# Attention with 16 queries a head: K of a block in one load of 64 KB rows, its last 28 tokens through a buffer of their own

## The chip, the core and the metric

The kernel runs on one core of a Trainium2 chip. The metric is device time in microseconds (us), the median of the runs; a profiled execution has a span, from its first to its last instruction. The engines are PE (TensorE, with PEld for its weight loads), DVE (VectorE), ACT (ScalarE), POOL (GpSimd) and SP (SyncE, which here only issues DMAs).

## The reference

For each of 8 x 16 = 128 heads there are 16 queries, 2048 keys and 2048 values of 256 numbers each, all in bf16.

```python
B, H, Sq, Skv, Dh = 8, 16, 16, 2048, 256
scores = jnp.einsum('bhqd,bhkd->bhqk', q, k) * q.shape[-1] ** -0.5
attn = softmax(scores, axis=-1)
out = jnp.einsum('bhqk,bhkd->bhqd', attn, v)
```

## The kernel before

**Blocks.** Eight heads make a block, so there are G = 16 blocks. K of a block is 8 MB, V as well. SBUF holds one block of K and one of V (the tile `SL`, four slots of 64 tokens a partition: `VA`, `VB` for V, `KA`, `KB` for K). V of a block comes as 128 tokens a partition, 16 partitions to a head, in rows of 64 KB. K comes in two halves of four heads, each 64 tokens a partition, 32 partitions to a head, in rows of 32 KB and loads of 4 MB. K of block 0 goes to V's slots, K of block 1 to K's.

**One block.** DVE transposes K in place, 32 tokens of all 256 numbers at a time (`kt`, line 200, 128x4096 words of 4 bytes). PE multiplies it with zero-padded query weights `QW` into `S_ps` (`qk`, lines 296 and 297: 296 with a weight load, 297 without). DVE takes the maximum (222), ACT the exponential (282), DVE transposes the result twice (226, 227), and DVE and ACT copy it into `PTz`, padded (207, 209 and 269). PE then multiplies it with V (`pv`, 317, "PV" below), and ACT writes the scaled result (262).

**Order.** Each engine has its own loop, written out by hand, over the blocks. PE's loop does QK of block r, 20 spare matmuls into `X_ps` that are used nowhere, and PV of block r-1. DVE's does the softmax of block g and the transposes of K of block g+1. Block 0 has its own QK loop ahead (328 to 337).

**Loads.** SP issues all DMAs on one queue, in program order, each behind a wait until its place is free: a half of K waits for the QK of that half of the block before it (`c_qk` grows by 4 a half, 8 a block), V for the end of the PV of the block before it (`c_pv`, 8 a block). The order is K halves of block j, then V of block j-1 (148 to 152); ahead of that loop, blocks 0 to 2 are written out (134 to 147), V of blocks 0 and 1 in halves. K and V of the last blocks come in smaller pieces (`PIECES`).

Of the kernel before, what the change touches and what calls it, by code (L numbers as in the profile page):

```python
# [5 lines left out]
ALU = mybir.AluOpType  # L6
# [4 lines left out]
SP = mybir.EngineType.SP  # L11
BF16 = mybir.dt.bfloat16
F32 = mybir.dt.float32

T = 64
SPARE = 5
# [4 lines left out]
def bass_standalone__softmax_full_bidir__sampling_kernel(  # L21
# [16 lines left out]
    ku = k.rearrange("b h s d -> (b h s) d").rearrange("(u p t) d -> u p t d", p=128, t=T)  # L38
# [4 lines left out]
    with ExitStack() as es:  # L43
        ec = es.enter_context
        SL = ec(nc.sbuf_tensor("SL", [128, 4, T, D], BF16))
        QT = ec(nc.sbuf_tensor("QT", [128, SQ * D], BF16))
# [19 lines left out]
        def sem(name):  # L66
            return ec(nc.semaphore(name))
# [3 lines left out]
        s_k = [sem("s_ka"), sem("s_kb")]  # L71
        s_kl = [sem("s_kla"), sem("s_klb")]
        s_v = sem("s_v")
        s_v0 = sem("s_v0")
# [6 lines left out]
        c_kt = [sem("c_kt0"), sem("c_kt1")]  # L81
# [10 lines left out]

        SLf = SL[:].bitcast(F32)

        QX = PTz[:, 1, 0:SQ * D // 128, :].rearrange("p t m -> p (t m)")

        QXu = QX.rearrange("p (c u a y) -> p a u c y", u=8, a=4, y=2)

        QTu = QT[:].rearrange("p (c u y) -> p u c y", u=32, y=2)

        SLk = SL[:].rearrange("p s (c t) (b i q) -> p s c b q t i", t=16, i=32, q=2)

# [5 lines left out]
        VW = SL[:, VA:VB + 1, :, :].rearrange("p a t d -> p (a t) d")  # L108


# [9 lines left out]
        def qx(Q, a):  # L120

            return (QTu[32 * a:32 * a + 32, 8 * Q:8 * Q + 8, :, :].rearrange("p u c y -> p c u y"),
                    QXu[32 * Q:32 * Q + 32, a, :, :, :].rearrange("p u c y -> p c u y"))

        def load_k(eng, g, e, slot, t0, n, s):
            eng.dma_start(SL[:, slot, t0:t0 + n, :], ku[2 * g + e, :, t0:t0 + n, :]).then_inc(s, 16)  # L126

        def on_sync(eng):
            def load_v(w, a, n):

                eng.wait_ge(c_pv, 8 * w + (a + n + C - 1) // C)
                eng.dma_start(VW[:, a:a + n, :], vb[w, :, a:a + n, :]).then_inc(s_p[a] if a else s_v, 16)  # L132

            eng.dma_start(QX, qh).then_inc(s_q, 16)
            for g, s0, s in ((0, VA, s_k0), (1, KA, s_k)):
                for e in range(2):
                    load_k(eng, g, e, s0 + e, 0, T, s[e])

            for e in range(2):
                eng.wait_ge(c_qk, 4 * e + 4)  # L140
                eng.dma_start(VW[:, T * e:T * e + T, :], vb[0, :, T * e:T * e + T, :]).then_inc(s_v0 if e else s_v, 16)
            for e in range(2):
                eng.wait_ge(c_qk, 4 * e + 12)
                load_k(eng, 2, e, KA + e, 0, T, s_k[e])
            for e in range(2):
                eng.wait_ge(c_pv, 4 * e + 12)
                eng.dma_start(VW[:, T * e:T * e + T, :], vb[1, :, T * e:T * e + T, :]).then_inc(s_v0 if e else s_v, 16)
            with nc.Fori(3, last, engines=[SP], hint_back_edge=True) as j:
                for e in range(2):
                    eng.wait_ge(c_qk, 8 * j + 4 * e - 4)  # L150
                    load_k(eng, j, e, KA + e, 0, T, s_k[e])
                load_v(j - 1, 0, 2 * T)
            for e in range(2):
                eng.wait_ge(c_qk, 8 * last + 4 * e - 4)
                load_k(eng, last, e, KA + e, 0, T // 2, s_k[e])
                load_k(eng, last, e, KA + e, T // 2, T // 2, s_kl[e])
            for w in PIECES:
                for a, n in PIECES[w]:
                    load_v(w, a, n)
            eng.wait_ge(c_ev, G)  # L160
            eng.dma_start(oh[:, 0:last, :], O_all[:, 2:G + 1, :]).then_inc(s_st, 16)
            eng.wait_ge(c_ev, G + 1)
            eng.dma_start(oh[:, last, :], O_all[:, G + 1, :]).then_inc(s_st, 16)
            eng.wait_ge(s_st, 32)

        def on_gpsimd(eng):

            for x, n in ([(c_pv, 8)] + [(x, 1) for x in s_kl] +
                         [(s_p[a], 16 * G - 16 * sum(a in dict(PIECES[w]) for w in PIECES)) for a in s_p]):
                eng.sem_inc(x, n)  # L170
# [18 lines left out]
            eng.memset(zero[1], 0.0).then_inc(c_pool, 1)  # L189

        def on_vector(eng):
# [6 lines left out]
            def kt(e, h, slot, n=1, first=False):  # L198
                x = SLf[:, slot, 32 * h:32 * h + 32 * n, :].rearrange("p t i -> p (t i)")
                eng.transpose(x, x).then_inc(c_k0 if first else c_kt[e], n)  # L200
# [11 lines left out]
            for e in range(2):  # L212
                eng.wait_ge(s_k0[e], 16)
                for h in range(2):
                    kt(e, h, VA + e, 1, True)

            eng.wait_ge(s_k[0], 16)
            kt(0, 0, KA, 2)
            eng.wait_ge(c_pool, 2)
            with nc.Fori(0, G, engines=[DVE]) as g:  # L220
# [8 lines left out]
                mid = eng.to_reg((g + 15) & 15)  # L229
                with eng.If_lt(mid, 14):  # L230
                    eng.wait_ge(s_k[0], 16 * g + 16)
                    kt(0, 0, KA)
# [3 lines left out]
                with eng.If_lt(mid, 14):  # L236
                    eng.wait_ge(s_kl[0], ((g + 2) & 16) + 1)
                    kt(0, 1, KA)
                gg = eng.to_reg(g)
                with eng.If_lt(gg, last):  # L240
                    eng.wait_ge(s_k[1], 16 * g + 16)
                    kt(1, 0, KB)
                    eng.wait_ge(s_kl[1], ((g + 2) & 16) + 1)
                    kt(1, 1, KB)
# [5 lines left out]
        def on_scalar(eng):  # L250
            def qwb(src):
                for a in range(4):
                    dv = QW[32 * a:32 * a + 32, :, 16 * a:16 * a + 64, :]
                    dv = bass.AP(tensor=dv.tensor, offset=QW[32 * a:32 * a + 32, 0, 16 * a, :].offset,
                                 ap=[list(dv.ap[0]), [1024 + 512, 2], [2, 64], [1, 2]])
                    eng.activation(dv, src(a), ACTF.Copy, scale=scale).then_inc(c_qw, 1)  # L256
# [17 lines left out]
            qwb(lambda a: QXu[0:32, a, 0:2, :, :])  # L274
            eng.wait_ge(c_pool, 2)
            with nc.Fori(0, G, engines=[ACT]) as g:
# [4 lines left out]
                sv = bass.AP(tensor=sv.tensor, offset=sv.offset, ap=[list(sv.ap[0]), [32, 64], [1, 2], [2, 16]])  # L281
# [10 lines left out]
        def on_tensor(eng):  # L292
# [9 lines left out]
            def qk(e, cs, slot):  # L302
                for bp in range(8):
                    for c in cs:
                        ins = mm(S_ps[:, c, :], QW[:, e, :, bp], SLk[:, slot, c, bp // 2, bp % 2, :, :],
                                 e == 0 and bp == 0, e == 1 and bp == 7, c == cs[0])
                return ins

            def pv(rr, two):

                for t in range(2 * T):
                    if t == T:
                        eng.wait_ge(s_v0, two)
                        eng.wait_ge(c_co[1], 8 * r + 1)
# [13 lines left out]
            with nc.Fori(0, 2, engines=[PE]) as e:  # L328
                for h in range(2):
                    with nc.Fori(0, 4, engines=[PE]) as b:  # L330
                        eng.wait_ge(c_k0, 2 * e + h + 1)
                        for par in range(2):
                            for c in (2 * h, 2 * h + 1):
                                ins = mm(S_ps[:, c, :], QW[:, e, :, 2 * b + par], SLk[:, VA + e, c, b, par, :, :],
                                         False, False, c == 2 * h, False)
                        if h:
                            ins.then_inc(c_qk, 1)

            two = eng.alloc_register("two")
            with nc.Fori(1, G + 1, engines=[PE], hint_back_edge=True) as r:  # L340
                rr = eng.to_reg(r)
                r16 = eng.to_reg(16 * r)
                with eng.If_lt(rr, G):
                    for e in range(2):
                        for h in range(2):
                            eng.wait_ge(c_kt[e], 2 * r + h - 1)
                            if e + h == 0:
                                eng.wait_ge(c_ex, rr)
                            ins = qk(e, (2 * h, 2 * h + 1), KA + e)
                        ins.then_inc(c_qk, 4)  # L350

                    mid = eng.to_reg((r + 14) & 15)
                    with eng.If_lt(mid, 13):
                        with nc.Fori(0, SPARE, engines=[PE]) as x:
                            for _ in range(4):
                                mm(X_ps[:], QW[:, 1, :, 7], QT[:, 0:512], True, True, False)
# [3 lines left out]
                eng.reg_alu(two, r16, 32, ALU.min)  # L360
                pv(r16, two)
# [34 lines left out]
```

## Time and profile before

| | us |
|---|---|
| runs | 631.23, 631.26, 631.54; median 631.26 |
| span of the profiled execution | 630.1 |
| PE busy | 535.6 (85%) |
| DVE busy | 419.4 (67%) |
| ACT busy | 269.1 (43%) |
| POOL busy | 26.0 (4%) |
| DMA moved | 270.54 MB, mean 429 GB/s |

The profiled execution's own time is its span; what lies around the span in a run brings it to the time that is measured. Busy times of engines overlap, and a busy PE is not PE at its peak. The share of the DMA queue is the time its packets took, over 16 engines and the span. "PEclk" is the clock that PE was granted. A row of the chain gives start, length and what ended the wait; "issue" is time without a visible wait.

### The profile page before, as it was taken

The numbers are of one execution on the slowest core, as the hardware profiler recorded it, in microseconds if no ns is written. First come the engines' busy times: TensorE is split into PE (matmuls) and PEld (weight loads), VectorE is DVE, ScalarE is ACT, GpSimd is POOL, SyncE is SP. The second block draws the span as 40 slices with busy tenths as digits, with TensorE's granted clock in tenths as the row PEclk, the third lists the DMA queues.
The fourth block names the chain that finished last, engine by engine and source line by source line (L and its number), as shares of the span: only waits on it lengthen the run. The fifth ranks groups of instructions, "written<-read, shape, count | busy, mean of one in ns | idle before, by whom it ended". The sixth has DMA issues, their size and how long they took to land.

```text
span 630.1 us, 7710 instructions
## 1 busy us (share of the span) xinstructions
PE 535.6 (85%) x3336; PEld 273.4 (43%) x2561; DVE 419.4 (67%) x193; ACT 269.1 (43%) x308; POOL 26.0 (4%) x30
## 2 busy tenths in 40 slices
PE   1658989889888898888978889888889878899997
PEld 0112734518244272542726336263362724518386
DVE  1989694865849657496574956749566594768740
ACT  1016562723437243362534525335263352732653
POOL 7800000000000000000000000000000000000000
PEclk9998989999899998999999899999998999999999
DMA  9999999999999999999999999999999999999999
GB/s 377 433 435 431 433 431 424 433 439 426 466 399 466 408 433 441 424 441 424 437 453 408 458 408 458 416 424 441 424 441 449 408 458 408 458 404 421 435 428 376
DMA packets 11008, 270.54 MB, mean 429 GB/s; under 512 B 1024, under 2 KB 3072, under 8 KB 3584
## 3 DMA queue, kind: packets, MB, share of 16 engines
q1 hardware_dynamic: 11008, 270.54, 99.9%
HBM read 269.48 MB, written 1.05 MB: 429 GB/s over the span
## 4 chain that ended last, share of the span: by engine, by line
DMA 57%; PE 34%; issue 4%; DVE 4%; SPq 0%; DVEq 0%; ACT 0%
DMA SL<-in_v_dram 52%; PE O_ps L317 30%; DMA SL<-in_k_dram 5%; DVE SL L200 2%; PE S_ps L296 1%; PE S_ps L297 1%; DVE PTb L227 1%; DVE negm L222 1%; PE X_ps L297 1%; SPq L132 0%; DVE PTz L207 0%; DVE PTz L209 0%; SPq L126 0%; ACT P_sb L282 0%; DVE O_all L247 0%
## 5 line engine op out<-in xcount | busy, mean ns | idle before, releaser
L200 DVE STREAM_TRANSPOSE SL<-SL 128x4096 f32<-128x4096 f32 (+1 forms) x63 | 280.6, 4492 | 88.1 <-DMA SL<-in_k_dram 87.6
L296 PE MATMUL S_ps<-SL,QW 128*128 128x512 bf16 (+1 forms) x512 | 206.1, 403 | 57.6 <-DVE SL L200 48.9
L317 PEld LDWEIGHTS O_ps<-SL,PTz 128*128 128x128 bf16 x2048 | 198.9, 98 | 114.2 <-issue 89.0
L317 PE MATMUL O_ps<-SL,PTz 128*128 128x256 bf16 x2048 | 226.6, 273 | 24.9 <-DMA SL<-in_v_dram 23.8
L297 PE MATMUL S_ps<-SL,QW 128*128 128x512 bf16 (+1 forms) x512 | 205.6, 401 | 0.0
L296 PEld LDWEIGHTS S_ps<-SL,QW 128*128 128x128 bf16 (+1 forms) x512 | 74.4, 145 | 230.1 <-issue 161.9
L256 ACT ACTIVATE QW<-QT 32x256 bf16 x64 | 26.9, 420 | 168.5 <-PE S_ps L297 167.3
L269 ACT ACTIVATE PTz<-PTa 16x1024 bf16<-16x1024 bf16 x32 | 33.8, 1056 | 128.9 <-PE O_ps L317 114.2
L222 DVE TENSOR_REDUCE negm<-S_ps 128x1 f32<-128x2048 f32 x16 | 36.6, 2289 | 58.3 <-PE S_ps L297 58.3
L269 ACT ACTIVATE PTz<-PTa,mk 32x1024 bf16<-32x1024 bf16 x64 | 72.3, 1130 | 0.0
L269 ACT ACTIVATE PTz<-PTb 16x1024 bf16<-16x1024 bf16 x64 | 67.2, 1051 | 1.2
L226 DVE STREAM_TRANSPOSE PTa<-P_sb 128x2048 bf16<-128x2048 bf16 x16 | 37.0, 2312 | 35.4 <-ACT P_sb L282 35.4
L297 PE MATMUL X_ps<-QT,QW 128*128 128x512 bf16 x260 | 58.2, 379 | 0.0
L227 DVE STREAM_TRANSPOSE PTb<-P_sb 128x2080 bf16<-128x2080 bf16 x16 | 36.8, 2302 | 0.0
L269 ACT ACTIVATE PTz<-PTb,mk 32x1024 bf16<-32x1024 bf16 x32 | 36.2, 1132 | 0.0
L282 ACT ACTIVATE P_sb<-S_ps,negm 128x2048 bf16<-128x2048 f32 x16 | 31.5, 1967 | 5.9 <-DVE negm L222 5.9
L262 ACT ACTIVATE O_all<-O_ps,rinv 128x256 f32 x15 | 7.1, 473 | 39.8 <-PE O_ps L317 39.8
L184 POOL COPY QT<-PTz 32x1024 bf16<-32x1024 bf16 x16 | 17.4, 1087 | 2.4 <-DVE PTz L194 1.5
L207 DVE TENSOR_SCALAR PTz<-PTb,mk 32x1024 bf16<-32x1024 bf16 x32 | 15.2, 476 | 0.0
L209 DVE COPY PTz<-PTa 16x1024 bf16<-16x1024 bf16 x32 | 13.5, 422 | 1.1
L247 DVE TENSOR_SCALAR O_all<-O_ps,rinv 128x256 bf16<-128x256 f32 x1 | 0.5, 484 | 20.4 <-PE O_ps L317 20.4
L296 PE MATMUL S_ps<-PTz 128*128 128x512 bf16 x1 | 0.6, 608 | 9.9 <-ACT QW L256 9.9
(18 smaller groups left out, 21.0 us busy)
## 6 DMA issues: line engine op xcount, KB each, us to landing
SL<-in_k_dram SPq DMA_DIRECT2D x30, 4096.0 KB, 24.2
SL<-in_v_dram SPq DMA_DIRECT2D x4, 4096.0 KB, 21.3
SL<-in_k_dram SPq DMA_DIRECT2D x4, 2048.0 KB, 21.5
SL<-in_v_dram SPq DMA_DIRECT2D x1, 3840.0 KB, 21.3
SL<-in_v_dram SPq DMA_DIRECT2D x1, 2496.0 KB, 22.0
SL<-in_v_dram SPq DMA_DIRECT2D x1, 2048.0 KB, 12.2
SL<-in_v_dram SPq DMA_DIRECT2D x1, 1856.0 KB, 24.7
SL<-in_v_dram SPq DMA_DIRECT2D x1, 1792.0 KB, 10.8
```

The costliest lines, as they stand in the source:

```text
L184: eng.tensor_copy(*qx(n // 4, n % 4)).then_inc(c_cq, 1)
L200: eng.transpose(x, x).then_inc(c_k0 if first else c_kt[e], n)
L207: ins = eng.tensor_scalar(out=dst, in0=src, scalar1=m, scalar2=None, op0=ALU.mult)
L222: eng.tensor_reduce(out=negm[:], in_=S_ps[:].rearrange("p c n -> p (c n)"), axis=AX.X, op=ALU.max, negate=True).then_inc(c_mx, 1)
L226: eng.transpose(fa[:, 0:2048], P_sb[:, 16:2064]).then_inc(c_pt, 1)
L227: eng.transpose(fb[:, 0:2080], P_sb[:, 0:2080]).then_inc(c_pt, 1)
L256: eng.activation(dv, src(a), ACTF.Copy, scale=scale).then_inc(c_qw, 1)
L269: eng.activation(dst, src, ACTF.Copy, scale=m if x else 1.0).then_inc(c_co[e], 1)
L282: eng.activation(P_sb[:, 16:2064], sv, ACTF.Exp, bias=negm[:], scale=1.0, accum_out=lsum[:]).then_inc(c_ex, 1)
L296: return eng.matmul(dst, w, x, start=start, stop=stop, skip_group_check=not check)
L297: return eng.add_instruction(mybir.InstMatmult(name=nc.get_next_instruction_name(), engine=PE, start_tensor_calc=start, stop_tensor_calc=stop,
L317: ins = eng.matmul(O_ps[:, 0:D], PTz[:, t // T, t % T, :], VW[:, t, :], start=(t == 0), stop=(t == 2 * T - 1))
```

## The change

K of a block is laid out as V is: 128 tokens a partition, 16 partitions to a head. For blocks 2 to 13 it comes in one load of 8 MB with rows of 64 KB (`load_k` into `KW`), and V of blocks 0 and 1 comes in one load too. K of blocks 0, 1 and 14 still comes in two halves, now of 64 tokens of all heads; K of block 15 comes in four pieces.

GpSimd copies tokens 100 to 127 of a block (28 of them, `TX` = 100), in two copies of 14 tokens, to the new buffer `KX`, once K has landed. DVE transposes K in pieces of 32, 32, 20 and 16 tokens in place and the 28 tokens in `KX`. PE does QK in five parts to match, each part for the two heads of a group of 32 partitions in turn (e = 0, 1): 16 matmuls of 512, 512 and 320 columns, 16 pairs of 192 and 64, and 16 of 448 out of `KX`. `c_qk` grows by 4 after the fourth part and by 4 after the fifth. The next K load waits for the fourth part and for GpSimd's copies (`c_x`). Ahead of the loop DVE transposes 32 tokens of K of block 1; it was 64. The spare matmuls stand ahead of the QK and wait for K's load. The score columns, and with them the views of `QW`, `QT` and `S_ps`, are rearranged to suit; the numbers of elements are the same.

The diff, cut to its core:

```diff
-    ku = k.rearrange("b h s d -> (b h s) d").rearrange("(u p t) d -> u p t d", p=128, t=T)
+    kb = k.rearrange("b h s d -> (b h s) d").rearrange("(g p t) d -> g p t d", p=128, t=2 * T)
...
+        KX = ec(nc.sbuf_tensor("KX", [128, 2 * T - TX, D], BF16))
...
+        VW, KW = block(VA), block(KA)
+        VS, KS, XS = split(VW), split(KW), split(KX[:])
...
-        def load_k(eng, g, e, slot, t0, n, s):
-            eng.dma_start(SL[:, slot, t0:t0 + n, :], ku[2 * g + e, :, t0:t0 + n, :]).then_inc(s, 16)
+        def load_k(eng, g, dst, t0, n, s):
+            eng.dma_start(dst[:, t0:t0 + n, :], kb[g, :, t0:t0 + n, :]).then_inc(s, 16)
...
+            for e in range(2):
+                load_k(eng, 0, VW, T * e, T, s_k0[e])
             for e in range(2):
-                eng.wait_ge(c_qk, 4 * e + 4)
-                eng.dma_start(VW[:, T * e:T * e + T, :], vb[0, :, T * e:T * e + T, :]).then_inc(s_v0 if e else s_v, 16)
+                load_k(eng, 1, KW, T * e, T, s_kl if e else s_k)
+            eng.wait_ge(c_qk, 8)
+            eng.dma_start(VW, vb[0]).then_inc(s_v, 16)
+            with nc.Fori(2, last - 1, engines=[SP], hint_back_edge=True) as j:
+                eng.wait_ge(c_qk, 8 * j - 4)
+                eng.wait_ge(c_x, 2 * j - 2)
+                load_k(eng, j, KW, 0, 2 * T, s_k)
+                load_v(j - 1, 0, 2 * T)
+            eng.wait_ge(c_qk, 8 * last - 12)
+            eng.wait_ge(c_x, 2 * last - 4)
             for e in range(2):
-                eng.wait_ge(c_qk, 4 * e + 12)
-                load_k(eng, 2, e, KA + e, 0, T, s_k[e])
...
+                load_k(eng, last - 1, KW, T * e, T, s_kl if e else s_k)
+            load_v(last - 2, 0, 2 * T)
+            eng.wait_ge(c_qk, 8 * last - 4)
+            eng.wait_ge(c_x, 2 * last - 2)
+            for t0, t1, x in ((0, 32, s_k), (32, T, s_kp[0]), (T, TX, s_kp[1]), (TX, 2 * T, s_kp[2])):
+                load_k(eng, last, KW, t0, t1 - t0, x)
...
+            half = (2 * T - TX) // 2
+            with nc.Fori(1, last, engines=[POOL]) as n:
+                eng.wait_ge(c_qk, 8 * n)
+                eng.wait_ge(s_k, 16 * n)
+                eng.wait_ge(s_kl, ((n + 2) & 16) + 16)
+                eng.sem_inc(c_mk, 1)
+                for e in range(2):
+                    eng.tensor_copy(KX[:, half * e:half * e + half, :].rearrange("p t d -> p (t d)"),
+                                    KW[:, TX + half * e:TX + half * e + half, :].rearrange("p t d -> p (t d)")).then_inc(c_x, 1)
...
-            eng.wait_ge(s_k[0], 16)
-            kt(0, 0, KA, 2)
+            eng.wait_ge(s_k, 16)
+            kt(KW, 0, 32)
...
                 copies(0, (2, 3))
-                with eng.If_lt(mid, 14):
-                    eng.wait_ge(s_kl[0], ((g + 2) & 16) + 1)
-                    kt(0, 1, KA)
+                mid = eng.to_reg((g + 15) & 15)
+                with eng.If_lt(mid, last - 2):
+                    eng.wait_ge(s_k, 16 * g + 16)
+                    kt(KW, 0, 32)
                 gg = eng.to_reg(g)
-                with eng.If_lt(gg, last):
...
+                with eng.If_lt(gg, last - 1):
+                    kt(KW, 32, T)
+                    eng.wait_ge(s_kl, ((g + 3) & 16) + 16)
+                    kt(KW, T, 84)
+                    kt(KW, 84, TX)
+                    eng.wait_ge(c_x, 2 * g + 2)
+                    kt(KX, 0, 2 * T - TX)
...
+            def qk(parts, n):
+                for e in range(2):
+                    for bp in range(8):
+                        for x, c, t, t0, t1 in parts:
+                            ins = mm(S_ps[:, c, 16 * t:16 * (t + t1 - t0)], QW[:, e, :, bp],
+                                     x[:, t0:t1, bp // 2, 16 * e:16 * e + 16, bp % 2],
+                                     e + bp == 0, e == 1 and bp == 7, t0 == parts[0][3])
+                if n:
+                    ins.then_inc(c_qk, n)
...
+                mid = eng.to_reg((r + 14) & 15)
+                with eng.If_lt(mid, last - 3):
+                    with nc.Fori(0, SPARE, engines=[PE]) as x:
+                        eng.wait_ge(s_k, r16)
+                        for _ in range(4):
+                            mm(X_ps[:], QW[:, 1, :, 7], QT[:, 0:512], True, True, False)
                 with eng.If_lt(rr, G):
...
+                    for i, (parts, n) in enumerate((
+                            ([(KS, 0, 0, 0, 32)], 0), ([(KS, 1, 0, 32, T)], 0), ([(KS, 2, 0, T, 84)], 0),
+                            ([(KS, 2, 20, 84, 96), (KS, 3, 0, 96, TX)], 4),
+                            ([(XS, 3, TX - 96, 0, 2 * T - TX)], 4))):
+                        eng.wait_ge(c_kt, 5 * r - 4 + i)
+                        if i == 0:
+                            eng.wait_ge(c_ex, rr)
+                        qk(parts, n)
```

On SP, from V of block 0 to the end of the loop, a row names the line, the tile, the shape and, in brackets, what is waited for. Before:

```order
L141 DMA SL<-in_v_dram 128x16384 [waits c_qk] x2
L126 DMA SL<-in_k_dram 128x16384 [waits c_qk] x2
L147 DMA SL<-in_v_dram 128x16384 [waits c_pv] x2
L148 UNCONDITIONAL_BRANCH
L148 BRANCH_PREFETCH_HINT
L148 ISA
L126 ISA [waits c_qk]
L126 DMA SL<-in_k_dram 128x16384
L126 ISA [waits c_qk]
L126 DMA SL<-in_k_dram 128x16384
L131 ISA
```

After, in the same place:

```order
L147 DMA SL<-in_v_dram 128x32768 [waits c_qk]
L148 UNCONDITIONAL_BRANCH
L148 BRANCH_PREFETCH_HINT
L148 ISA
L150 ISA [waits c_qk]
L133 ISA [waits c_x]
L133 DMA SL<-in_k_dram 128x32768
L138 ISA
L139 ISA [waits c_pv]
L139 DMA SL<-in_v_dram 128x32768
```

The halves of K of block 2 and of V of blocks 0 and 1 are gone from ahead of the loop; the loop starts with block 2, and its K load has two waits and one DMA of 128x32768.

On DVE, from the last copies into `PTz` in a round to the end of the transposes of K for the next block. Before:

```order
L209 COPY PTz<-PTa 16x64x16
L207 TENSOR_SCALAR PTz<-PTb,mk 32x64x16
L236 COMPARE_AND_BRANCH
L237 REGISTER_ALU x2
L200 STREAM_TRANSPOSE SL<-SL 128x4096 [waits s_kla]
L236 UNCONDITIONAL_BRANCH
L240 COMPARE_AND_BRANCH
L241 ISA
L200 STREAM_TRANSPOSE SL<-SL 128x4096 [waits s_kb]
L243 REGISTER_ALU x2
L200 STREAM_TRANSPOSE SL<-SL 128x4096 [waits s_klb]
```

After:

```order
L221 TENSOR_SCALAR PTz<-PTb,mk 32x64x16
L250 REGISTER_ALU x2
L251 COMPARE_AND_BRANCH
L252 ISA
L214 STREAM_TRANSPOSE SL<-SL 128x4096 [waits s_k]
L251 UNCONDITIONAL_BRANCH
L255 COMPARE_AND_BRANCH
L214 STREAM_TRANSPOSE SL<-SL 128x4096
L257 REGISTER_ALU x3
L214 STREAM_TRANSPOSE SL<-SL 128x2560 [waits s_kl]
L214 STREAM_TRANSPOSE SL<-SL 128x2048
L214 STREAM_TRANSPOSE KX<-KX 128x3584 [waits c_x]
```

The transposes of K, one of which stood ahead of the copies (in the rows above these), now all stand behind them, and they are five: the third waits for `s_kl`, the one in `KX` for GpSimd's copies.

On PE, a round of block 0's QK loop (ISA and REGISTER_ALU compute addresses). Before:

```order
L330 ISA
L296 ISA [waits c_k0]
L296 ISA
L296 MATMUL S_ps<-SL,QW 128x512
L300 ISA
L297 MATMUL S_ps<-SL,QW 128x512
L296 ISA
L296 REGISTER_ALU
L296 MATMUL S_ps<-SL,QW 128x512
L300 ISA
L297 MATMUL S_ps<-SL,QW 128x512
L330 REGISTER_ALU
```

After:

```order
L322 ISA [waits c_k0]
L322 REGISTER_ALU
L322 MATMUL S_ps<-SL,QW 128x512
L322 ISA
L322 MATMUL S_ps<-SL,QW 128x512
L322 ISA
L322 MATMUL S_ps<-SL,QW 128x512
L322 ISA
L322 MATMUL S_ps<-SL,QW 128x512
L357 REGISTER_ALU
L357 COMPARE_AND_BRANCH
```

A round keeps its four matmuls; before, two of them (297) reuse the weights of the matmul ahead, after, each loads its own (322). Six ISA instructions became four.

More of the change, by code (lines that the diff above doesn't have):

```diff
@@ L15 @@
 T = 64
+TX = 100
 SPARE = 5
@@ L327, in on_tensor @@
                 mm(S_ps[:, c, :], PTz[:, 0, 0, :], PTz[:, 0, 0:4, :].rearrange("p t m -> p (t m)"), True, False, c == 0, False)
[L328 to L339, printed above, removed]
+            for c in range(4):
+                with nc.Fori(0, 4, engines=[PE]) as b:
+                    eng.wait_ge(c_k0, c + 1)
+                    for par in range(2):
+                        for e in range(2):
+                            ins = mm(S_ps[:, c, :], QW[:, e, :, 2 * b + par],
+                                     VS[:, 32 * c:32 * c + 32, b, 16 * e:16 * e + 16, par],
+                                     False, False, True, False)
+                    if c > 1:
+                        ins.then_inc(c_qk, 1)
             with nc.Fori(1, G + 1, engines=[PE], hint_back_edge=True) as r:
@@ L359, in on_tensor @@
                 eng.wait_ge(s_v, r16)
-                eng.reg_alu(two, r16, 32, ALU.min)
-                pv(r16, two)
+                pv(r16)
         on_sync(nc.sync)
```

101 lines of the change are left out of this document (39 added, 62 removed).

## The prediction

> **What bounds the kernel now.** I read the page's queue table first, then the chain that ended last in the middle of the run, then the landings of single loads.
>
> ```profile
> span 630.1 us, 7710 instructions
> ...
> q1 hardware_dynamic: 11008, 270.54, 99.9%
> ```
>
> The packets fill the 16 DMA engines for 99.9% of the span. So every pause of the queue adds its own length to the time, and compute counts only where it makes a load late. The chain between two V loads shows how late they are:
>
> ```profile
> 311.34 24.24 DMA SL<-in_v_dram
> 335.58 0.23 issue
> 335.81 14.15 PE O_ps L317 x128
> ...
> 350.12 24.23 DMA SL<-in_v_dram
> ```
>
> A V load is issued when the PV of the block ahead ends (349.96) and lands 24.23 us later, at 374.35. The K halves of that round, by the page of K's load line cut to each half (duration, start; then time to landing), are issued at 321.1 and 329.8:
>
> ```profile
> L126 SPq DMA_DIRECT2D SL<-in_k_dram x1: 333/333/333, 321.1 to 321.1; - x1
> ...
> L126 SPq DMA_DIRECT2D SL<-in_k_dram x1: 333/333/333, 329.8 to 329.8; - x1
> ...
> DMA to landing us min/median/max: 25.2/25.2/25.2
> ```
>
> The second half lands at 355.0. So the queue brings V by 335.58, K by 355.0 (19.42 us for two halves of 4 MB), V by 374.35 (19.35 us for one load of 8 MB). A V load moves for 19.35 of its 24.23 us, so it queues for 4.9 us; the first K half queues for longer still. Nothing starves, and a round of 38.77 us is pure transfer.
>
> **What the longer rows are worth.** 19.42 less 19.35 is 0.07 us for each pair of halves that becomes one load; rounding of the landings leaves 0 to 0.15. K of blocks 2 to 13 and V of blocks 0 and 1 become such loads: 14 x 0.07 = 1.0 us less (0 to 2.1). The last two blocks keep as many K loads as before.
>
> **What one load costs at the head.** Before, K of block 2 goes out in halves:
>
> ```profile
> L141 SPq DMA_DIRECT2D SL<-in_v_dram x2: 328/328/328, 31.4 to 43.2; - x2
> ...
> DMA to landing us min/median/max: 20.8/21.8/22.8
> ```
>
> ```profile
> L126 SPq DMA_DIRECT2D SL<-in_k_dram x2: 328/328/328, 57.6 to 67.0; - x2
> ...
> DMA to landing us min/median/max: 16.1/16.3/16.4
> ```
>
> V of block 0 lands at 43.2 + 20.8 = 64.0. The first K half, issued at 57.6, is waiting behind it and lands at 73.7, 9.7 us later: no pause. The second half, issued at 67.0, hides behind the first. After the change there is no first half: the whole load waits for the fourth QK part of block 1 (c_qk 12). I follow that chain on the clock of before, by timeline rows (start, us, engine, line; in brackets the wait ahead).
>
> ```profile
> 48.08 0.62 PE L296 MATMUL S_ps<-SL,QW 128*128 128x512 bf16 x1 [4.94 <-ACT P_sb L282]
> 48.49 0.63 PE L297 MATMUL S_ps<-SL,QW 128*128 128x512 bf16 x1
> ...
> 53.91 0.48 DVE L207 TENSOR_SCALAR PTz<-PTb,mk 32x1024 bf16<-32x1024 bf16 x1
> 54.42 8.77 DVE L200 STREAM_TRANSPOSE SL<-SL 128x4096 f32<-128x4096 f32 x2
> ...
> 58.93 0.44 PE L296 MATMUL S_ps<-SL,QW 128*128 128x512 bf16 x1 [1.40 <-DVE SL L200]
> ```
>
> ```profile
> 34.95 8.71 DVE L200 STREAM_TRANSPOSE SL<-SL 128x8192 f32<-128x8192 f32 x1 [1.01 <-DMA SL<-in_k_dram]
> ...
> 290.68 4.48 PE L297 MATMUL X_ps<-QT,QW 128*128 128x512 bf16 x20
> ```
>
> Before, 64 tokens of K of block 1 are transposed ahead of the loop (the 8.71 us row, while DVE would wait anyway); after, only 32. Tokens 32 to 63 come behind the four copies that end at 54.4: 4.4 us, to 58.8. Then 20 tokens (2560 words at 8.71/8192 = 1.06 ns, with issue 2.75 us) to 61.6, and 16 tokens (2.2 us) to 63.8. On PE the second part, 16 matmuls of 512 columns, starts at 58.9; at 4.48/20 = 0.22 us each it takes 3.5. The third, 320 columns, takes 16 x 0.14 = 2.2. The fourth, 192 + 64 columns, takes 16 x 0.11 = 1.8 (a PV matmul of 256 columns takes 14.15/128 = 0.11). At full clock the parts end at 62.4, 64.6, 66.4.
>
> Full clock is not to be had there. The first part has 16 matmuls now, not 32; it ends near 53.7, and PE waits 5.2 us for the second. A wait of 4.94 us, in the first row above, was followed by matmuls 0.43 apart. In two stretches of PE (length, busy, granted clock, DMA share, GB/s), and in a timeline row, one sees why:
>
> ```profile
> 46.00:52.60 6.60, 4.52 (x11) 0.50 1.02 442
> ...
> 86.90:90.20 3.30, 3.30 (x9) 0.50 1.04 447
> ...
> 86.70 0.59 PE L296 MATMUL S_ps<-SL,QW 128*128 128x512 bf16 x1 [2.21 <-DVE SL L200]
> ```
>
> The clock column reads 0.50 to 52.6 there, 4.5 us into the work, and for 3.4 us in a second case behind a wait of only 2.21. Of the second part I put 3 us at half clock, which adds 1.5 (bounds 0 and 2.3): the parts end at 63.9, 66.1 and 67.9, and the load is issued 0.3 later, at 68.2. The Trainium skill, "TensorE: Matmul & The Clock Gate", Part 1, says that PE falls to half clock after an idle window of about 3.4 us and returns after a busy one; by it the addition would be 1.7 us and the sum 0.2 higher. The two rows of 0.50 agree with its clock and length, but the wait of 2.21 us shows that less than its window of idling suffices.
>
> The start of this chain may move too. Block 0's QK loop is paced by register work, as the rows of its lines show (shortest, median, longest ns, first and last start):
>
> ```profile
> L330 PEldq FUSED_REGOPS  x8: 50/50/50, 31.7 to 41.6; - x8
> ...
> L296 PEldq FUSED_REGOPS  x27: 102/138/143, 30.0 to 42.2; - x27
> ```
>
> Its rounds are 9.9/7 = 1.41 us for four matmuls of 0.22. A round has six address instructions, two sums and a branch; after the change four address instructions, all of the long kind (0.138), two sums and a branch, but four weight loads for two. Scaled by instruction it comes to 1.28, or 0 to 2.1 us less over 16 rounds. I take 0.6: the first four rounds go by matmuls at half clock, and the added weight loads give part of it back. The issue is then at 67.6.
>
> A load into an empty queue also has a lead time; the page's DMA issues give the KB and the us to landing:
>
> ```profile
> PTz<-in_q_dram SPq DMA_DIRECT2D x1, 1024.0 KB, 5.0
> ...
> out_dram<-O_all SPq DMA_DIRECT2D x1, 64.0 KB, 1.6
> ```
>
> The 64 KB store lands 1.6 us after issue, 1.45 without its own transfer at 429 GB/s; the q load of 1 MB has 2.6 to spare. I take 1.5, from the store, since the queue was already in use. So the queue pauses for 67.6 + 1.5 - 64.0 = 5.1 us. Bounds: with full clock and 2.1 us of earlier start, DVE's fourth piece and the part behind it allow an issue at 63.8 - 2.1 + 1.8 + 0.3 = 63.8 and a pause of 1.2; with 4.6 us of half clock, no earlier start and 2.6 of lead, 69.0 + 2.6 - 64.0 = 7.6. V of block 0, now one load at 43.2 or a little earlier, meets the end of block 1's K (64.0 - 19.4 = 44.6) within its lead: nothing.
>
> **What hides in the later rounds.** Count from K's landing at 355.0; V ends 19.35 later, so K of the next block must be issued by 17.85. DVE: pieces of 4.4, 4.4, 2.75 and 2.2, done at 13.8. PE: the 20 spare matmuls, now behind K's semaphore, run to 4.5; the parts end at 8.0, 12.4, 14.6 and 16.4, issue at 16.7: 1.1 us in hand. PE is now idle for about 3.6 us ahead of the spares, since PV ends later; with 3.4 us of half clock the chain is 1.7 later ahead of the first part, issue at 17.5, 0.35 in hand. Cost nothing, but the cover is thin. V: GpSimd's 28 tokens are transposed by 17.7 and used by 20.9, PV follows for 14.15, V is issued at 35.4 with 1.5 lead, against K's end at 38.7: covered.
>
> ```profile
> L184 POOL COPY QT<-PTz x16: 1066/1086/1120, 8.2 to 25.4; 32x1024 bf16<-32x1024 bf16 x16
> ...
> 15.46 8.77 DVE L200 STREAM_TRANSPOSE SL<-SL 128x4096 f32<-128x4096 f32 x2 [7.36 <-DMA SL<-in_k_dram]
> ...
> 25.17 8.77 DVE L200 STREAM_TRANSPOSE SL<-SL 128x4096 f32<-128x4096 f32 x2 [0.94 <-DMA SL<-in_k_dram]
> ```
>
> GpSimd's copies took at most 1.12 us for 1024 elements, beside DVE transposes and alone. Two of 3584 are 7.6 to 7.8 us: done 8 us after K's landing, long before DVE asks at 13.8 or SP at 16.7; in block 1 done near 52.4, before DVE's copies. Even doubled they end ahead of SP's wait. The altered reads of S_ps and writes of QW keep their element counts: nothing, hidden by the queue. The tail's V pieces are the same and go behind 77 us of queue: nothing.
>
> **Sum.** 5.1 - 1.0 = 4.1 us on the profiled span of 630.1 gives 634.2. The median of the runs, 631.26, stands 1.2 over that span; so 635.3.
>
> **Rivals.** *The rounds starve too.* If the fourth part (two small matmuls to each weight load) takes 0.17 us a time, not 0.11, it lasts 1.0 longer; rounds with half clock are then 0.65 late. Eight of 12 such rounds cost 5 us: 640.5. It decides where the issue passes 17.85. For it: the margin of 0.35. Against: PV already runs a load and a matmul in 0.11 us.
>
> *The head's pause vanishes (not slower).* If block 0's loop ran at its matmuls' pace, 4 x 0.22, it would end four rounds behind DVE's transpose of block 0's last quarter (25.17 + 8.77 = 33.9, so 37.5) and not at 43.2; that takes 5.7 us off, and the time would be 631.26 - 1.0 = 630.3. It decides where the loop ends by 39.8. For it: fewer register instructions. Against: those left are the long ones, and need 1.28 us a round.
>
> *Each load's fixed cost is saved.* The other mechanism for a gain: merging 14 pairs saves 14 fixed costs. The pairs above show 0.07 us each, so at most 2.1 us in all, and with no pause 629.2. The Trainium skill, "SBUF — State Buffer", "The DMA setup-cost knee", puts a roughly fixed 2 us on every transfer; an estimate by it is 28 us saved, 603. The trace contradicts that for queued loads: 19.42 against 19.35.
>
> **How the numbers follow.** The pause at the head alone: 70 in 100, 635.3, its own range 632.6 to 638.9 (below, full clock and a start 1.8 earlier take 2.7 off the pause; above, a pause of 7.6 and no gain). Starving rounds: 15, near 640.5. No pause: 10. Fixed cost saved: 3. Others: 2. What a measurement can tell is 0.2%, 1.3 us. No pause gives "same" (630.3 is 1.0 below), the saved fixed costs "faster" with half of the others; the rest is slower: 86 slower, 10 same, 4 faster. The range from 632.6 to 640 leaves out the cases without a pause and half of the starving ones, under 2 in 10.
>
> **What would show it.** In the profile after: K of block 2 issued near 67 to 68 with nothing ahead of it, landing some 21 us later; a slice near 65 us with a low DMA share; rounds of 38.7 us behind it; K's issue 16.7 to 17.5 us behind K's landing; copies on POOL near 3.8 us each. I am wrong if block 0's QK ends before 40, if rounds are over 38.8 us, or if the DMA share stays at 99.9%.

## The result, and the profile after

| | median us | runs from, to | ratio to before (95% interval) |
|---|---|---|---|
| before | 631.33 | 631.23, 631.61 | |
| after | 664.57 | 663.03, 667.87 | 1.0535 (1.0515 to 1.0556) |

The change costs 33 us. 635.3 was forecast, with a range of 632.6 to 640: the direction was right, the size far too small. The profiled execution took 663.03 us; its span is 31.6 us longer than before. The page's lines on the span and the DMA queues:

```profile
span 661.7 us, 9014 instructions
...
q1 hardware_dynamic: 8992, 270.54, 96.3%
```

The same bytes fill the queue for 96.3% of the span, not 99.9%: it now pauses for some 24 us. The other 7.8 us of the 31.6 are packets that take longer: in the load of 352.93, shown below, the first packet on each of the 16 engines takes 2.75 to 3.51 us, the next one 2.42. The chain that ended last shows where the queue pauses, in a round in the middle of the run (start, length, what):

```profile
352.93 21.90 DMA SL<-in_k_dram
374.83 0.04 issue
374.87 6.99 PE X_ps L323 x20
381.86 9.44 PE S_ps L322 x49
391.30 0.03 PE S_ps L323
...
393.55 0.05 PE S_ps L323
...
393.85 21.95 DMA SL<-in_k_dram
```

Before, this chain ran from V load to PV to V load. Now it runs from one K load to the next: K lands at 374.83, the spare matmuls take 7.0 us, the first three parts of QK 9.4, the fourth 2.3, and the next K load is issued at 393.85, 19.0 us behind the landing. A round takes 40.9 us (38.77 before). The V load in front of the K load of 352.93, and that K load, by the rows of their two lines (duration ns, start; time to landing):

```profile
L139 SPq DMA_DIRECT2D SL<-in_v_dram x1: 332/332/332, 329.0 to 329.0; - x1
...
DMA to landing us min/median/max: 24.4/24.4/24.4
```

```profile
L133 SPq DMA_DIRECT2D SL<-in_k_dram x1: 333/333/333, 352.9 to 352.9; - x1
...
DMA to landing us min/median/max: 21.9/21.9/21.9
```

V lands at 353.3, so K is issued 0.4 us ahead of the end of the queue. It lands 21.5 us behind V, where 8 MB need 19.35: 2.1 us are lost here, and 1.7 to 2.3 in the other rounds.

At the head, the loads of V of block 0 and of K of block 2:

```profile
L147 SPq DMA_DIRECT2D SL<-in_v_dram x1: 328/328/328, 39.2 to 39.2; - x1
...
DMA to landing us min/median/max: 24.8/24.8/24.8
```

```profile
L133 SPq DMA_DIRECT2D SL<-in_k_dram x1: 342/342/342, 68.3 to 68.3; - x1
...
DMA to landing us min/median/max: 21.8/21.8/21.8
```

V lands at 63.9, K is issued 4.4 us later and lands at 90.1, 26.2 us behind V: a pause of 6.85 us, 4.4 of waiting and 2.4 for the start of the load. The sum, by landings:

| | us later than before, in all |
|---|---|
| K of block 2 (90.1, before 83.4) | 6.7 |
| K of block 13, 11 rounds on (538.4, before 510.1) | 28.3, so 1.97 a round |
| K of block 14, again issued late | 30.2 |
| V of block 13 | 30.7 |
| span | 31.6 |

### The profile page after: what moved, and what is told of

Read it like the earlier page. It is cut to its first block, busy times and chain, and to the rows that moved or that the text cites. A ratio compares the mean times of both kernels' runs of the same rounds, so it can differ in the third digit from the quotient of the medians.

```text
span 661.7 us, 9014 instructions
## 1 busy us (share of the span) xinstructions
PE 556.1 (84%) x3796; PEld 381.4 (58%) x3313; DVE 421.6 (64%) x209; ACT 268.9 (41%) x308; POOL 113.2 (17%) x58
## 3 DMA queue, kind: packets, MB, share of 16 engines
q1 hardware_dynamic: 8992, 270.54, 96.3%
## 4 chain that ended last, share of the span: by engine, by line
DMA 48%; PE 46%; issue 2%; DVE 2%; ACT 1%; SPq 0%; DVEq 0%; ACTq 0%
DMA SL<-in_k_dram 45%; PE S_ps L322 25%; PE X_ps L323 12%; PE O_ps L345 8%; DMA SL<-in_v_dram 4%; ACT PTz L295 1%; PE S_ps L323 1%; DVE SL L214 1%; DVE PTb L241 0%; DVE negm L236 0%; SPq L133 0%; DVE PTz L221 0%; DVE O_all L273 0%; ACT O_all L288 0%; SPq L150 0%
## 5 line engine op out<-in xcount | busy, mean ns | idle before, releaser
L214 DVE STREAM_TRANSPOSE SL<-SL 128x4096 f32<-128x4096 f32 (+1 forms) x64 | 223.2, 3541 | 109.9 <-DMA SL<-in_k_dram 109.8
L322 PEld LDWEIGHTS S_ps<-SL,QW 128*128 128x128 bf16 (+1 forms) x1024 | 147.3, 145 | 221.3 <-issue 170.8
L322 PE MATMUL S_ps<-SL,QW 128*128 128x512 bf16 (+3 forms) x1024 | 201.4, 348 | 22.8 <-DVE SL L214 17.4
L202 POOL COPY KX<-SL 128x3584 bf16<-128x3584 bf16 x28 | 88.0, 3173 | 468.2 <-DMA SL<-in_k_dram 468.2
L323 PE MATMUL X_ps<-QT,QW 128*128 128x512 bf16 x240 | 81.5, 517 | 61.7 <-DMA SL<-in_k_dram 61.7
L214 DVE STREAM_TRANSPOSE KX<-KX 128x3584 f32<-128x3584 f32 x14 | 54.2, 3873 | 0.5 <-POOL KX L202 0.5
L322 PE MATMUL S_ps<-KX,QW 128*128 128x448 bf16 x240 | 49.7, 357 | 1.0 <-DVE KX L214 1.0
L322 PEld LDWEIGHTS S_ps<-KX,QW 128*128 128x128 bf16 x240 | 33.4, 146 | 12.0 <-DVE KX L214 1.2
L323 PE MATMUL S_ps<-SL,QW 128*128 128x64 bf16 x240 | 36.7, 191 | 0.0
L223 DVE COPY PTz<-PTa 16x1024 bf16<-16x1024 bf16 x32 | 15.9, 498 | 1.7
## 6 DMA issues: line engine op xcount, KB each, us to landing
SL<-in_k_dram SPq DMA_DIRECT2D x2, 2048.0 KB, 17.5
SL<-in_v_dram SPq DMA_DIRECT2D x1, 1856.0 KB, 23.5
```

The costliest lines, as they stand in the source:

```text
L202: eng.tensor_copy(KX[:, half * e:half * e + half, :].rearrange("p t d -> p (t d)"), KW[:, TX + half * e:TX + half * e + half, :].rearrange ...
L214: eng.transpose(x if dst is None else words(dst), x).then_inc(s, 1)
L322: return eng.matmul(dst, w, x, start=start, stop=stop, skip_group_check=not check)
L323: return eng.add_instruction(mybir.InstMatmult(name=nc.get_next_instruction_name(), engine=PE, start_tensor_calc=start, stop_tensor_calc=stop,
```

## The experiments

The losses have two places, the head and the rounds. The first theory on the rounds was: a load that is issued as the queue runs dry pays some 2.5 us, and K comes so late because PE idles ahead of the spare matmuls and then runs at half clock. Each text below says what its theories mean.

**No spare matmuls.** All of them are left out of the rounds.

```diff
-                with eng.If_lt(mid, last - 3):
-                    with nc.Fori(0, SPARE, engines=[PE]) as x:
...
```

> The changed kernel without the spare matmuls. Theory A (a round is K's load into an empty queue, 21.9 us, then on PE the 20 spare matmuls, 7.0 us of which most at half clock, then four QK parts, 11.8 us, then the issue): the first part starts at DVE's first piece, 4.5 us behind K's landing and not 7.0, but then it takes the half clock itself, 0.6 to 2.3 us longer. Rounds of 38.9 to 40.6 us, not 40.95, so 640 to 661 us, about 651. Theory B (GpSimd's copies or DVE's pieces set the round): 664 us as it was.

665.55 us, 1.0535 (1.0518 to 1.0553): no gain. Theory A is missed and theory B's time is near; whether GpSimd sets the round is asked below. The chain of its waits:

```profile
355.70 21.91 DMA SL<-in_k_dram
...
377.64 4.46 DVE SL L214
...
382.14 11.95 PE S_ps L322 x49
...
396.64 21.78 DMA SL<-in_k_dram
```

PE starts QK 4.5 us behind the landing, as soon as DVE has the first piece, but the half clock moves with it: the 49 matmuls take 11.95 us for 9.4. The issue is 19.0 us behind the landing again, so this run doesn't yet tell what half clock costs.

**Spare matmuls that don't wait for K.** 36 of them run through PE's idle time.

```diff
-                    with nc.Fori(0, SPARE, engines=[PE]) as x:
-                        eng.wait_ge(s_k, r16)
+                    with nc.Fori(0, 9, engines=[PE]) as x:
```

> The changed kernel with 36 spare matmuls for 20, and without their wait for K's load: they fill PE from the end of PV to the first piece of K. Theory A: PE is at full clock and free when the first piece comes (4.5 us behind the landing), the fourth part ends near 17.0, the load is issued before the queue runs dry; rounds of 38.7 us, and only the pause at the head (6.7 us) stays: 637 to 640 us. Theory B (GpSimd or DVE set the round): 664 us.

661.1 us, 1.0471 (1.0454 to 1.0489): 3.5 us less, far from theory A's 637 to 640. Four of its five runs took 660.9 to 661.6 us; the profiled one took 666.4, so its rounds are likely longer than theirs. Its chain:

```profile
386.26 6.10 PE S_ps L322 x33
...
394.90 23.70 DMA SL<-in_k_dram
```

PE is at full clock now, and K goes out 17.5 us behind its landing (377.4), which is what the prediction had: about 1.9 us ahead of V's end. The load then takes 23.7 us, and the rounds are 40.9 us on average. 1.5 us of earlier issue in a round bought nothing in the profiled execution and 3.5 us in all in the median. So the half clock makes up little of the loss, and here an earlier issue does not take its own length off it.

**No copies on GpSimd.** DVE transposes tokens 100 to 127 straight from `KW` into `KX`, and the K load waits for that.

```diff
-                eng.wait_ge(c_x, 2 * j - 2)
+                eng.wait_ge(c_kt, 5 * j - 5)
...
-                    eng.wait_ge(c_x, 2 * g + 2)
-                    kt(KX, 0, 2 * T - TX)
+                    kt(KW, TX, 2 * T, dst=KX[:])
```

> The changed kernel without GpSimd's copies: DVE transposes the 28 tokens straight from K's place into KX, and the next K load waits for that transpose (done near 17.8 us behind the landing) in place of GpSimd. Theory A: PE's chain (issue 19.0 us behind the landing) is the longer one, so the rounds stay at 40.95; at the head DVE's copy takes 0.42 us again, not 2.90, which can bring the K load of block 2 up to 2.5 us forward: 661 to 665 us. Theory B, GpSimd sets the round: 640 us or below.

660.98 us, 1.0466 (1.0443 to 1.049), at the lower edge of theory A and far from theory B. By its chain K of block 2 goes out 2.8 us earlier, and the rounds are as long as they were (41.0):

```profile
65.54 21.89 DMA SL<-in_k_dram
...
349.80 21.86 DMA SL<-in_k_dram
...
390.79 21.93 DMA SL<-in_k_dram
```

So GpSimd's copies cost 3 us once, at the head, and nothing in the rounds.

**K in two halves again.** Blocks 2 to 13 load tokens 0 to 63 and 64 to 127 apart, one behind the other; all else stays.

```diff
-                load_k(eng, j, KW, 0, 2 * T, s_k)
+                load_k(eng, j, KW, 0, T, s_k)
+                load_k(eng, j, KW, T, T, s_kl)
...
```

> The changed kernel with K of blocks 2 to 13 in two loads of 4 MB (tokens 0 to 63, then 64 to 127, rows of 32 KB) issued together, each with a semaphore of its own; all else as changed. Theory A: DVE and the spares start 9.7 us earlier in a round, the fourth part ends about 12.5 us behind K's landing, no load is late; rounds of 38.78 us and the head's pause alone: 637 to 639 us. Theory C (the five-part QK or the new layout is what is slow on PE): rounds stay over 40 us, 655 us or more.

647.27 us, 1.0249 (1.0231 to 1.0266): 17 of the 33 us, and between the two theories. DVE can begin when the first half has landed, so K is issued in time. Its chain is now one of V loads:

```profile
362.65 23.36 DMA SL<-in_v_dram
...
386.14 16.80 PE O_ps L346 x128
...
403.10 21.81 DMA SL<-in_v_dram
```

PV takes 16.8 us for 14.15, part of it at half clock, because the spare matmuls stand ahead of QK and PE idles ahead of PV. V is then the load that is late.

**Halves, with the spare matmuls behind QK,** where they were before.

```diff
                         qk(parts, n)
+                    mid = eng.to_reg((r + 14) & 15)
+                    with eng.If_lt(mid, 13):
+                        with nc.Fori(0, SPARE, engines=[PE]) as x:
...
```

> Starts from the kernel with K of blocks 2 to 13 in two halves of 4 MB (647.3 us) and moves the 20 spare matmuls back behind QK, ahead of PV, without their wait for K. Theory A (there the V load was late only because PE idles ahead of PV and runs it at half clock, 16.8 us): PV takes 14.2 us, V is issued over 4.5 us ahead of the end of K, rounds take 38.8 us, and only the pause at the head (6.7 us, less 1 us for the merged V loads) is left: 636 to 638 us. Rival B (V is late because the last of the five QK parts comes too late behind K's landing, whatever the clock): 645 us or more.

638.17 us, 1.0112 (1.0095 to 1.0129), within 0.2 us of theory A. PV by the timeline, and five V loads of the middle:

```profile
341.17 14.14 PE L346 MATMUL O_ps<-SL,PTz 128*128 128x256 bf16 x128
```

```profile
L139 SPq DMA_DIRECT2D SL<-in_v_dram x5: 332/332/333, 316.6 to 471.8; - x5
...
DMA to landing us min/median/max: 24.3/24.3/24.4
```

They are issued (471.8 - 316.6)/4 = 38.8 us apart, 5 us ahead of the queue's end. The rounds lose nothing. The head is left, where the first half of K of block 2 lands 15.15 us behind V of block 0 and not 9.7: 5.4 of the 5.9 us that this span is longer than before.

**How far ahead must a load be issued?** This was asked of the kernel before, where nothing else moves. Both K halves of blocks 3 to 14 wait for the row maximum of the block ahead (first run) or for its exponentials (second).

```diff
-                    eng.wait_ge(c_qk, 8 * j + 4 * e - 4)
+                    eng.wait_ge(c_mx, j)        # second run: c_ex, j
```

> The kernel before, but in blocks 3 to 14 both K halves are issued when the row maximum of the block ahead is done (both QK halves are read by then): about 3.1 us ahead of the end of the V load in front, where before it was 14.5 and 5.8. Nothing else moves. Theory A (a load that is issued less than some 3.5 to 5 us before the queue runs dry pays part of its start-up): 0 to 1 us a round, 12 rounds, 631 to 643 us. Rival B (the lead of 1.5 us in the prediction's sum): no change, 631.3 us.

> The kernel before, but in blocks 3 to 14 both K halves are issued when the exponentials of the block ahead are done: about 1.3 us ahead of the end of the V load in front. Nothing else moves. Theory A (start-up of 2 to 2.5 us for such a load, though it is issued while the one in front still moves): 1.5 to 2.5 us a round, 12 rounds, 649 to 661 us. Rival B (the lead of 1.5 us in the prediction's sum): 0.2 us a round, 634 us.

643.4 us, 1.0201 (1.0172 to 1.0231), for the maximum, and 660.05, 1.0456 (1.043 to 1.0482), for the exponentials: the first is 0.4 us above theory A's range, the second inside it, and the lead of 1.5 us would have given 631.3 and 634. Of the second, two V loads from the chain and the K half behind each:

```profile
239.65 26.19 DMA SL<-in_v_dram
...
282.04 25.78 DMA SL<-in_v_dram
```

```profile
L126 SPq DMA_DIRECT2D SL<-in_k_dram x1: 333/333/333, 264.3 to 264.3; - x1
...
DMA to landing us min/median/max: 14.5/14.5/14.5
```

```profile
L126 SPq DMA_DIRECT2D SL<-in_k_dram x1: 333/333/333, 306.5 to 306.5; - x1
...
DMA to landing us min/median/max: 12.5/12.5/12.5
```

V ends at 265.84 and 307.82, so the halves are issued 1.5 and 1.3 us ahead. They land 13.0 and 11.2 us behind V for 9.7. These runs reproduce the loss of the change in a kernel that has none of its other parts.

**Fewer spare matmuls.** 12 for 20, in the changed kernel. Its rounds and those without spare matmuls had both come to 12 x 3.413 us, the length of the stretches in which the granted clock changes; so a rival was that they settle on it.

```diff
-SPARE = 5
+SPARE = 3
```

> The changed kernel with 12 spare matmuls a round for 20. Theory A (issue and start-up add up freely: 8 matmuls less at 0.22 to 0.43 us take 1.8 to 3.4 us off the time from K's landing to the next issue, which is then 1.9 to 3.6 us ahead of the V load's end, with 0.5 to 2.5 us of start-up): rounds of 39.2 to 40.5 us, 644 to 660 us. Rival B (the round settles on 12 windows of the clock gate, 12 x 3.413 = 40.96 us, whatever the number of spare matmuls; the half-clock windows move into QK): rounds of 40.96 us, 664 us.

663.01 us, 1.0511 (1.0495 to 1.0527). The time is the rival's, but not its mechanism: the rounds are no longer 40.96 us but scatter from 39.3 to 41.9. Two K loads from the chain:

```profile
391.48 24.20 DMA SL<-in_k_dram
...
433.17 21.79 DMA SL<-in_k_dram
```

Both are issued about 2 us ahead of V's landing; one loses 2.9 us, the other 0.2. By the packet records, the first packets of the 16 engines start 1.0 to 4.0 us behind the issue in the first case. In the changed kernel's load of 352.93 they all start 1.0 to 1.7 behind it. In the second case V itself ends unevenly. A load ends with one packet of 4 bytes on each engine, and it lands behind the last of them: 14 of the 16 engines had ended V 0.4 to 1.4 us before K was issued, and one only 1.9 us after. So "2 us ahead" holds for the last engine alone, and K seems to lose little because V landed late.

Together, for the loads of the middle rounds (issue against the landing of the load in front; loss is the landing beyond 19.35 us, or 9.71 for a half; the last column is the issue against the mean of the 16 engines' last packets of the load in front, negative where it comes behind them):

| kernel, loads | issued ahead, us | loss, us | mean loss | ahead of the engines' mean |
|---|---|---|---|---|
| no spare matmuls, 11 K | 0.0 to 0.4 | 2.1 to 2.6 | 2.3 | -0.5 |
| after, 11 K | 0.3 to 1.3 | 1.7 to 2.3 | 2.1 | -0.2 |
| before, behind the exponentials, 11 K halves | 1.3 to 1.8 | 1.4 to 3.5 | 2.2 | -0.2 |
| spare matmuls that don't wait, 11 K | 0.5 to 2.2 | 0.5 to 3.3 | 2.1 | 0.0 |
| 12 spare matmuls, 11 K | 1.7 to 2.2 | 0.2 to 3.3 | 1.9 | 0.4 |
| halves, 11 V that are issued late | 2.5 to 3.7 | 0 to 2.3 | 0.8 | 1.8 |
| before, behind the maximum, 11 K halves | 3.4 to 3.7 | 0 to 1.5 | 0.9 | 1.9 |
| halves, spare matmuls behind, 11 V | 3.8 to 5.0 | 0 to 0.2 | 0.02 | 4.2 |
| before, 12 V | 4.7 to 4.9 | 0 | 0 | 4.0 |

By the landing the loss looks flat from 0 to 2 us ahead. By the engines' mean it is not: over the loads of all these runs it is 2.3 us at 0.3 to 0.6 behind, 1.8 at 0 to 0.3 ahead, 1.3 at 1.0 to 1.3 ahead, and 0.1 from 2.4 ahead on. The two runs with an earlier issue gained so little because their engines end V 1.8 us apart on average, for 0.8 in the changed kernel, so that the landing came later than most of the engines' ends.

**The head.** DVE transposes tokens 32 to 63 of block 1's K ahead of its loop, as before, in the changed kernel.

```diff
             kt(KW, 0, 32)
+            kt(KW, 32, T)
             eng.wait_ge(c_pool, 2)
...
```

> Starts from the changed kernel; VectorE transposes tokens 32 to 63 of block 1's K ahead of its loop again, where it waits anyway, and not in the loop's first round. Theory A (K of block 2 is issued late because that piece stands behind block 0's copies, and the head's pause is part of the time): K of block 2 is issued near 61 us instead of 68.3 and lands some 6 us earlier; rounds stay at 40.95: 658 to 660 us. Rival B (the rounds follow the clock's 3.4 us windows so that a shift at the head is swallowed by the next round): within 2 us of 664.6.

659.86 us, 1.0448 (1.0423 to 1.0474): 4.7 less than after, as theory A said. K of block 2 goes out at 62.5 and lands at 85.0, 5.1 us earlier; the rounds stay as they are. V of block 0 lands at 65.8 here, for 63.9; more on this below.

**Both repairs, and an earlier first half.** Halves with the spare matmuls behind QK and the head's transpose ahead of the loop; then also the first half of K issued once tokens 0 to 63 are read.

```diff
-                eng.wait_ge(c_qk, 8 * j - 4)
-                eng.wait_ge(c_x, 2 * j - 2)
+                eng.wait_ge(c_qk, 8 * j - 6)
                 load_k(eng, j, KW, 0, T, s_k)
+                eng.wait_ge(c_qk, 8 * j - 4)
+                eng.wait_ge(c_x, 2 * j - 2)
                 load_k(eng, j, KW, T, T, s_kl)
...
```

In this version `c_qk` grows by 2 behind the second part of QK and by 2 behind the fourth.

> The two edits together: K of blocks 2 to 13 in halves with the spare matmuls back behind QK (638.2 us), and tokens 32 to 63 of block 1's K transposed ahead of VectorE's loop. Theory A (the losses add: the head's pause falls from 5.4 us to 0 to 1 us, since the first half of K of block 2 is issued near 61 to 62 us, some 2 us ahead of the end of V of block 0): 632 to 634 us. Rival B (the head's pause is not the remaining loss): 637 us or more.

> As the kernel with halves, spare matmuls behind QK and the head's transpose ahead of the loop, and the first K half is issued once tokens 0 to 63 are read, ahead of the rest of QK. Every load is now issued over 4 us ahead of the end of the one in front. Theory A (that lead is all that was lost): no pause anywhere, 631.3 us less at most 1 us for the merged V loads of blocks 0 and 1 (2 x 0.07 us) and whatever the longer rows give: 630.5 to 631.5 us, the same as before within what can be told. Rival B (rows of 64 KB, GpSimd's copies or the five QK parts cost something of their own): 633 us or more.

632.77 us, 1.0027 (1.0018 to 1.0036), and 632.71, 1.003 (1.0017 to 1.0042). So 31.8 of the 33 us are found again (theory A of the first), and the version with every load in time is still 1.4 us slower than before, outside what either of its theories said. Its page and the load of V of block 0:

```profile
q1 hardware_dynamic: 10720, 270.54, 99.8%
q8 instruction: 1, 0.02, 0.0%
```

```profile
L147 SPq DMA_DIRECT2D SL<-in_v_dram x1: 327/327/327, 39.1 to 39.1; - x1
...
DMA to landing us min/median/max: 26.3/26.3/26.3
```

This V load is issued 5.4 us ahead of the queue's end and yet lands at 65.4, 1.5 us late; from there on one or two of the 16 DMA engines end up to 1.7 us behind the first to the end, where before it was 0.8. A packet of 16 KB of instructions, of 1.06 us on one engine, lies at 63.27; the kernel before has none there. One engine's last packet of V comes where this packet ends, at 64.32; the other 15 ended V by 63.44. In the first of the two kernels and in the one with only the head's transpose moved, the same packet likewise ends where the last engine's V does, and V of block 0 takes 1.4 and 1.8 us too long. In the changed kernel the packet falls into the head's pause. So it holds up the landing of that V. That it is also the 1.4 us at the end fits in time and size, but no run took it away: it stays open. No version beat the kernel before, and what there is to gain, by the landings of pairs and single loads, is still 0.07 us a load.

## Why the prediction was wrong

**The step that failed: the lead of a load.** The sum took 1.5 us, from the 64 KB store, as all that a load must be issued ahead of the landing in front, and so found "1.1 us in hand" or "0.35 in hand" in the rounds. Counted from the landing, an 8 MB load loses about 2 us on average whether it is issued 0 or 2 us ahead; only from 3.8 us on is it free. Two things are in this: a late start costs more than 1.5 us (1.8 with the engines' mean end 0 to 0.3 us off), and a landing tells of the last engine, while the others have run dry up to 3 us before. The forecast issue at 16.7 to 17.5 us behind K's landing lies 1.9 to 2.7 us ahead of V's end, in or at the edge of that stretch. The run with full clock had just that issue (17.5 us in most rounds) and lost 2.1 a round. By the sum's own limit of 17.85 the issue measured in the changed kernel, 19.0, would have cost 1.2. 11 rounds and the load of block 14 make 23.5 of the 31.6 us. Since 13.8 us of DVE's transposes and the fourth part stand between landing and issue, a single K load at `TX` = 100 goes out at 16.4 us at best, 3 us ahead: an estimate from these rows, and by the table such loads lose 0.8 to 0.9 us on average.

**Half clock in the rounds.** Forecast 1.7 us from 3.4 us at half clock; the spare matmuls take 7.0 for 4.5, so 2.5. The idle time of 5.1 us ahead of them (forecast 3.6) is longer too. Wrong in size, but with little effect: the run at full clock is only 3.5 us faster.

**The fourth part** takes 2.3 us at 0.15 a pair, not 1.8. The prediction's rival of starving rounds named a mechanism of this kind, with 0.17 a pair and 5 us in all. The effect was there, nearly five times as large, and for the lead's sake. GpSimd's copies took 3.17 us each, below the 3.8 that were forecast.

**The head.** Issue at 68.3 for 67.6, pause 6.85 for 5.1; the term is near by luck, because its errors cancel. Block 0's QK loop ended near 39, not 42.6: its last 32 matmuls took 9.26 us, 1.16 a round of four, below the 1.28 that was scaled from instructions. So the condition of the rival without a pause (39.8) was met, and yet the pause came. By the sum's own terms a loop that ends 3.5 us earlier leaves 1.6 us of pause; the rest came from four terms that were too small. (A slip without effect: the lower bound of the pause is 63.8 + 1.5 - 64.0 = 1.3, not 1.2.) DVE and GpSimd in the changed kernel's timeline show the first reason:

```profile
44.72 6.28 POOL L202 COPY KX<-SL 128x3584 bf16<-128x3584 bf16 x2 [15.46 <-DMA SL<-in_k_dram]
```

```profile
48.38 2.90 DVE L223 COPY PTz<-PTa 16x1024 bf16<-16x1024 bf16 x1
...
51.71 0.42 DVE L223 COPY PTz<-PTa 16x1024 bf16<-16x1024 bf16 x1
```

DVE's copy into `PTz` takes 2.9 us beside GpSimd's copies, which end at 51.0, and ends 0.3 us behind them; the next takes 0.42. The prediction had them done "before DVE's copies", but the head ran 4 us earlier and they met. The Trainium skill, "SBUF — State Buffer", "Who interferes with whom", says that a DVE copy in a two-port mode and a GpSimd instruction hold a shared port in turn, and the later one blocks fully. The trace agrees: 2.9 for 0.42 us, while DVE's two transposes of the scores beside the same copies take 2.3 us each, as before the change. The second reason is PE's clock, in the chain:

```profile
52.56 4.46 DVE SL L214
...
57.07 8.72 PE S_ps L322 x33
...
68.34 21.77 DMA SL<-in_k_dram
```

The second and third part take 8.7 us, at a granted clock of 0.69 on average; 5.7 at full clock plus 1.5 was forecast. The start of the load took 2.4 us, not 1.5. So 2.5 for the copy, 1.5 for the two parts, 0.5 for the fourth and 0.9 for the start come on top of the 1.6: 7.0, for 6.85 measured.

**Right were:** the bound by the queue, the head's place and its cause (4.7 us came back with one piece of DVE's moved), 0.07 us as the worth of a merged load (V of block 0 lands 19.35 us behind K of block 1, for 19.43 before), and that fixed costs are not saved.

## What to carry to other kernels

Where one queue bounds the time, merging two loads takes away the first one, which covered the second's wait and start. Ask of every load how far ahead of the queue's end it is issued, and don't take the lead that it needs from a small store: here 1.5 us by the store was nearly 4 us by the landing in front, and loads issued later than that lost 0.8 to 2.3 us on average. The landing tells only when the last engine ends, so look at the others too. A repair that only moves the issue within that stretch shows little, so test the stretch by itself, in the kernel that has no loss.

## What was not expected of the hardware

- A load that is issued while the one in front still moves can lose nearly as much as one that is issued too late: counted from the landing, 2.3 us at 0 to 0.4 us ahead, 1.9 at 1.7 to 2.2, 0.9 at 3.4 to 3.7. Single loads scatter widely (0.2 to 3.3 at 2 us ahead). The start on the slowest of the 16 engines varies (1.7 and 4.0 us behind the issue in two of the loads above), and so does the end of the load in front (the engines end it 0.6 to 3.3 us apart in the run with 12 spare matmuls). Why a load that reaches its engines 1 us before they run dry still costs 1.3 us stays open.
- The rounds of some 40.95 us with 20 spare matmuls and with none look locked to 12 stretches of the clock (in both, half clock begins every 40.96 us by the records of the clock); with 12 they are not. Why the first two are so regular stays open.
